# A new hand-written order for the same tasks on five queues, and an x tile that is given back by whichever reader is last

## The chip, the cores and the metric

The kernel runs on one core of one Trainium2 chip. The metric is device time in microseconds (us) of one execution; the kernel before the change has a median of 258.22 us over three executions (257.47 to 258.88). All inputs and the output lie in device memory as float32. The core has a matrix engine (PE, which also has a row of its own for loading weights, PEld), three engines for elementwise work (DVE, ACT, POOL), and SP, which here only issues transfers and a few register loads.

## The reference

```python
# q, k, v: (4, 8, 768, 64); sampled_blocks: (24, 3); x tokens: 3072 of width 512; d_ff = 2048
mask = |i_block - j_block| <= 1, or either block is the first or last of 24, or j_block is sampled for i_block
attn = softmax(where(mask, q @ k.T / 8, -1e9)) @ v            # (4, 8, 768, 64), blocks of 32 rows
x    = attn.transpose(0, 2, 1, 3).reshape(3072, 512)
out  = (relu(x @ w_in) ** 2) @ w_out                          # w_in 512 x 2048, w_out 2048 x 512
```

## The kernel before, in words

**Tasks and the order.** The body first makes 1224 tasks (class Task). Each holds a function that emits a few instructions, the tasks that must stand before it, the buffers it takes (get) and the buffers it gives back (put). Then `run_program` (line 92) walks through a hand-written list, PROGRAM: a word such as `A246`, `V25` or `P231/2` names an engine (P = PE, V = DVE, A = ACT, G = POOL, S = SP's transfer queue), a task number and, for a task that writes PSUM, one of four PSUM banks X. The order of words is the order of instructions on each queue. Buffers other than the banks are dealt round robin: pT (8, the exponentials), r (3, relu results), g (12, squares), xT (4, transposed x), VG (3), KG (2), ys (2, output rows) and others. `run_program` asserts that a buffer is free, in program order, when the next task takes it. What has to wait in time is left to semaphores between the engines.

**Attention, batches 0 and 1** (units 0 to 7, each two heads). For each unit, 256 queries and two key chunks of 128, `scores` makes a 128x1024 bank of scores on PE (through `pair`, line 203: two matmuls of 64 rows), `exps` (L360, ACT) turns it into a pT tile, `masks` (L367, DVE) multiplies by a 0/1 mask tile (queries 0 to 255 have the mask added on PE instead), `values` or `values_full` (L203, L398) multiplies by V, `normalize` (L410 reciprocal, L413 multiply, both DVE) divides by the sums. The mask tiles come from PE through `mask_evac`, on ACT (L277) or on DVE (L279). In batch 0 the result is transposed on PE (L427) and copied to xT; in batch 1 it goes to the tile XS and is transposed by a DMA (L440).

**Attention, batches 2 and 3** (units 8 to 15) reads only the sampled key blocks, two block pairs per visit: `v_gather` (an indirect DMA on POOL, L579, or plain DMAs on SP, L582, whose addresses come from registers), `k_gather` (L593 to L599, copies on DVE or POOL whose addresses come from registers), `s_scores`, `s_exps` (L623, ACT), `s_masks` (L630, DVE), `s_values` (L653, PE), `s_normalize` (L659, L662, DVE), `s_transp` (L666, DMA). The sampled numbers pass once through a small table: `table_masks` writes the mask MKS (casts, L123, DVE), and `table_rows` computes row numbers (L524) and then loads the block numbers into registers on POOL, DVE and SP (L561, a TENSOR_LOAD).

**The feed-forward part** works in twelve tiles of 256 tokens. A tile has four groups of `hidden` (f = 0, 4, 8, 12; four parts of 8 matmuls each) that read its xT tile and w_in, then `relu` (L707 ACT or L709 DVE), `square` (L718 ACT or L720 POOL; two halves in the first tile and the last two), `output` (eight parts; matmuls with w_out), `out_copy` (L121, L123) and `store` (L771 to L781). The last tile's output is cut in four: 128 tokens whole, then 128 tokens by 256, 128 and 128 columns, 256, 128, 64 and 64 KB; the third of the four (i == 2) is issued on ACT's queue, all other stores on SP's.

**Casts and loads.** float32 inputs are cast to bf16 by `cast_qk` and `cast_v` on DVE, POOL or ACT (all through `copy`, L121 and L123). The weights are loaded in eight pieces by POOL's queue, and two small transfers on SP (S82, S83) wait for two of them before the later loads.

Of the kernel before, what the change touches and what calls it, by code (L numbers as in the profile page):

```python
# [25 lines left out]
def kernel(  # L26
# [22 lines left out]
    NF = d_ff // P  # L49
# [741 lines left out]
    ev, cv, cq, sc_of, va_of, mu, mk, wl, gate, xb = {}, {}, {}, {}, {}, {}, {}, {}, {}, {}  # L791
# [152 lines left out]
    for us in [range(b * HP, (b + 1) * HP) for b in range(B)]:  # L944
# [11 lines left out]
        if us[0] >= SB * HP:  # L956
            b = us[0] // HP
# [8 lines left out]
    for T in TILES:  # L966
        b, c0, tw = T
        n_u = per_unit(T)
        need = [mu[b * HP + a, c0] for a in range(HP)] if b < SB else [mu['s', b, c0 // P + i] for i in range(2)]
        for f in range(0, NF, n_u):  # L970
# [17 lines left out]
        for i, y in enumerate(ys):  # L988
# [3 lines left out]
            for part in range(NY):  # L992
# [4 lines left out]
                           put=[gbuf[T, f] for f in fs if (T, f) in gbuf] if i == len(ys) - 1 and part >= NY // 2 else [])  # L997
# [4 lines left out]
        A29 G35 P4/3 V32 P30/0 P12/2 P14/3 P9/1 P5/1 V31 P33/1 V111 P36/3 P0/2 A37 V1 V34 P102/2 V209 V46 P47/0 P106/1 A103 V48 P104/3  # L1002
        V43 A107 P44/0 G57 P7/2 V45 A105 P58/1 V54 P113/0 V59 P55/2 A114 P117/3 G41 V56 P2/1 V67 A118 P115/2 V3 P108/0 A116 V64 P127/1
        V109 P10/3 P65/3 A128 P123/2 V66 A124 P68/1 P125/3 G75 V69 V63 P92/1 P110 A126 P133/2 G76 V112 A134 P137/3 G52 S28 S42 S18 S19
        V93 S20 P88/0 A138 G38 V155 V89 P84/1 P119/2 G74 V85 A60 P86/0 P39/3 P135/1 V120 G73 A87 V40 A136 P121 P61/0 G49 P129/3 V122
        V62 G77 V70 P176/2 P170/0 P139/1 A177 G81 V130 G80 A171 V140 P146/2 P131 V132 A147 P149/3 V172 P71/0 P141 V142 A150 V72 P50/2
        P173/1 V148 P781/0 A174 P782 V178 P189/3 P783 V51 A190 V175 P90/1 P15/2 P96/2 P784 V91 A97 P183/3 V151 A785 P94/2 P179/1 V95
        A184 G787 P143/0 P774/2 V180 P775 A144 V191 G78 P186/3 P181 P776 V182 A187 P777 V145 P157/0 V778 A786 P152/3 A158 P160/1 V188
        P788/2 A161 V153 P163/0 P789 V185 A164 P790 V162 P154 P217/1 P791 A156 V159 A218 P192/0 V165 P795/3 A792 V193 S82 P166/1 S83
        V296 V219 S53 S254 A779 G794 S253 P194 P100/2 A780 P796 V195 V167 A101 P214/0 P797 G793 A215 P168 P798 V169 P211/2 V799 P824/1  # L1010
        G79 A212 P825 P196/0 G256 V216 P826 A197 P199/3 P818/2 G801 S257 P827 A200 P819 V828 P202/0 A800 S261 P228/3 P820 G22 A203
        S262 P821 V213 P812/1 S269 A229 V822 P813 G258 P220/0 A829 P814 V201 P245/2 S259 P221 A246 V198 P815 P802/3 V222 A816 P231/2
        V266 P223 P803 A232 V204 S267 P239/1 V230 P804 A224 A240 V264 S270 P242/0 P205/2 V233 S265 A243 P225/1 P206 P805 V207 A226
        S277 V274 P288/0 S436 S255 P208 P806 V227 A289 S275 V247 P11/1 P291/1 A823 P234/0 V241 P807 A292 V210 V244 P98/2 P235 V272
        P808 A99 V236 A817 S273 P298/2 V290 P248/1 P237 A299 P809 V238 S278 V293 P285/0 S279 V300 P249 A810 P830/2 V250 P831 A286 V282
        P304/3 P251 P832 V260 A305 P301/0 V252 P833 S263 V287 P852/1 A302 S334 S283 V834 P853 P846/3 G280 P313/0 V303 P854 A314 P316/2
        S281 P855 P847 A317 V856 G284 P294/0 P848 A835 S271 P295 V306 P310/1 S21 P849 G268 V297 A311 P864/2 V318 P865 S440 A850 P307/0
        V315 P866 S438 A857 P308 G851 S446 P355/3 P867 V309 A356 P322/1 V868 P858/0 P859 A323 P349/3 V357 P325/2 P860 A350 V312 P861
        P836/1 V276 A326 V351 S456 P319/3 A862 P328/2 V327 S439 P320 S447 A329 V321 P352/0 P837 S811 V324 A353 S454 P339/2 V330 P838
        A340 V354 P331/3 P342/0 A869 S385 V341 P332 P358/2 V333 P839 A343 V23 S335 G441 P359 A863 P336/3 P361/0 G443 P840 A337 P841  # L1020
        G451 A362 S622 P364/3 G449 P842 A365 P373/0 G445 S450 P843 A374 G461 P870/3 A844 S444 P367/0 V338 P871 A368 V344 S463 P872
        V347 V360 S455 V366 S442 P376/0 P345/1 A377 V363 P379/2 P346 P873 S452 V348 A380 V369 P403/0 P874 A404 V375 S464 P370/2 V378
        P400/1 P393/0 V381 P371 A401 P875 V372 S471 S448 A394 V402 P382/1 P390/2 V405 P383 A391 P387/0 P876 V384 A388 V395 S386 P406/1
        P886/2 V392 A407 P887 V457 P427/0 P877 A428 V465 P24/1 P888 S497 S462 A878 G453 P889 V408 S458 P880/0 A890 P881 P430/3 S466
        P882 V27 G891 A431 P883 P409/2 A884 P926/3 V26 P927 A885 P410 G469 P415/0 V398 V25 P928 V411 G467 A416 P892/1 S608 V389 P424/2
        S879 P893 A425 P929 S468 V432 P894 A930 P895 V426 P396/0 S470 A896 P16/2 V429 P898/3 S845 P397 S616 A931 P418/2 P433/1 V399
        P899 V459 A419 P932/0 P933 V474 S460 P412/2 P900 A413 P901 V417 P934 A902 S473 P434 V420 P935 V435 P482/3 G903 P904/2 A483
        V936 A897 P492/1 P905 V414 A493 P914/3 G503 P915 P480/0 S499 S623 P421/1 A481 P916 S542 P422 P906 G472 V423 V484 P907 S437
        G937 P917 P487/1 P908 V918 A488 P477/1 P490/0 P909 G501 A478 V504 A491 P485/1 P920/3 A919 G543 V494 P921 V479 V621 P475/0 P910
        A486 G500 V489 V625 A476 P911 V613 P495/1 A912 G546 S632 S913 V547 P511/2 S607 P505/0 V496 P922 A512 S520 S502 P923 A506  # L1030
        P954/1 V924 G627 P955 P514/2 P508/0 P956 A515 V507 G524 P557/3 S545 P957 V513 A509 P948/2 A925 P949 S614 P938/0 G544 A558 S498
        P939 V516 A958 V525 P551/3 S523 P950 A552 P940 V510 P554/3 P951 A555 P548/1 P941 G589 S628 A549 P517/3 A952 P966/1 G959 V518
        A953 P967 P535/2 P942 V550 S519 A536 P529/3 P943 G521 S626 V559 P526/2 P944 V590 G522 A527 P945 V537 P968 V609 A946 P960/2
        P961 V556 A530 P969 V528 P532/0 P962 A970 S540 S615 V553 P963 S585 G586 S624 P988/3 A971 V964 P989 P560/1 A533 V531 P990 A965
        V534 P594/2 P994/0 V561 A595 P995 P991 G567 S562 P996 A992 P538/1 V619 V568 S631 A993 P597/3 P972/2 S606 V539 A598 P997 V596
        S541 P600/1 P973 A601 G587 P1000/3 A998 V617 S620 P974 G999 P975 S610 P572/1 P1001 A573 S630 P982/0 G637 P1002 S588 P1003
        P575/1 P983 V1004 A576 P976 V611 P984 P578/1 P569/3 P985 V629 S612 A570 P977 V599 A986 V633 P978 S563 G565 S618 A579 V602
# [51 lines left out]
```

## Time and profile before

One execution was profiled: it took 258.88 us as timed, and its span in the trace is 257.1 us, so 1.78 us lie outside the trace. The granted clock was 1.000.

| engine | busy, us | share of span | instructions |
|---|---|---|---|
| PE | 243.1 | 95% | 5265 |
| PEld | 182.1 | 71% | 5265 |
| ACT | 183.6 | 71% | 217 |
| DVE | 171.3 | 67% | 408 |
| POOL | 98.8 | 38% | 178 |

A row of the trace names a line, an engine, an operation and its tiles (out<-in) and how many instructions it stands for. "busy" counts a moment once even if several instructions overlap. Matmuls are pipelined: one lasts 269 ns for 256 columns, yet 14 of them in a row take 0.93 us from the first's start to the last's end. The share of busy time is a mean over stages whose limits differ, so a stage has to be read by itself. SPq, DVEq and ACTq are the engines' own queues, which issue transfers and register loads and are not counted as busy.

### The profile page before, as it was taken

The numbers are of one execution on the slowest core, as the hardware profiler recorded it, in microseconds if no ns is written. First come the engines' busy times: TensorE is split into PE (matmuls) and PEld (weight loads), VectorE is DVE, ScalarE is ACT, GpSimd is POOL, SyncE is SP. The second block draws the span as 40 slices with busy tenths as digits, with TensorE's granted clock in tenths as the row PEclk, the third lists the DMA queues.
The fourth block names the chain that finished last, engine by engine and source line by source line (L and its number), as shares of the span: only waits on it lengthen the run. The fifth ranks groups of instructions, "written<-read, shape, count | busy, mean of one in ns | idle before, by whom it ended". The sixth has DMA issues, their size and how long they took to land.

```text
span 257.1 us, 12061 instructions
## 1 busy us (share of the span) xinstructions
PE 243.1 (95%) x5265; PEld 182.1 (71%) x5265; DVE 171.3 (67%) x408; ACT 183.6 (71%) x217; POOL 98.8 (38%) x178
## 2 busy tenths in 40 slices
PE   7888999999999997998998999999999999999993
PEld 4667879678874677975864867866875677767683
DVE  7778988899889995969916756657536725730301
ACT  3899999998999797846783975675965286623640
POOL 3183247003316026198556314264357620412100
PEclk9999999999999999999999999999999999999999
DMA  6999989999999996999699779998474923044022
GB/s 200 374 250 207 206 205 155 270 202 252 250 281 179 197 202 153 340 229 154 188 243 202 194 174 167 251 214 199 129 206 95 189 40 60 5 121 148 23 86 83
DMA packets 64692, 47.08 MB, mean 183 GB/s; under 512 B 31567, under 2 KB 60624, under 8 KB 64640
## 3 DMA queue, kind: packets, MB, share of 16 engines
q1 hardware_dynamic: 58512, 37.82, 64.7%
q0 software_dynamic: 5440, 8.05, 16.8%
q8 instruction: 41, 0.67, 1.1%
q10 hardware_dynamic: 688, 0.46, 0.6%
q14 instruction: 11, 0.09, 0.1%
HBM read 35.51 MB, written 7.91 MB: 169 GB/s over the span
## 4 chain that ended last, share of the span: by engine, by line
PE 53%; DVE 5%; DVEq 1%; issue 1%; ACT 1%; ACTq 0%
PE X L203 49%; PE X L653 4%; DVE VB L123 1%; ACT pT L623 1%; DVEq L561 1%; DVE MKS L123 1%; DVE pT L630 1%; DVE r L709 0%; DVE KG L599 0%; DVE qc L123 0%; DVE XS L413 0%; DVE KG L593 0%; DVE XS L662 0%; DVEq L599 0%; DVE rs L410 0%
## 5 line engine op out<-in xcount | busy, mean ns | idle before, releaser
L203 PE MATMUL X<-xT,w_in_sb 64*128 64x256 bf16 x1536 | 100.8, 269 | 2.8 <-issue 1.5
L203 PE MATMUL X<-w_out_sb,g 64*128 64x512 bf16 (+3 forms) x960 | 95.2, 334 | 0.1
L203 PEld LDWEIGHTS <-w_in_sb 64*128 64x128 bf16 x1536 | 74.6, 94 | 16.0 <-issue 5.4
L360 ACT ACTIVATE pT<-X 128x1024 bf16<-128x1024 f32 x72 | 70.6, 1030 | 7.6 <-PE X L203 6.8
L623 ACT ACTIVATE pT<-X 128x768 bf16<-128x768 f32 (+1 forms) x56 | 41.6, 766 | 26.5 <-PE X L203 23.9
L203 PEld LDWEIGHTS <-g 64*128 64x128 bf16 x960 | 40.3, 94 | 26.3 <-PE X L203 0.4
L720 POOL TENSOR_TENSOR g<-r 128x1024 bf16<-128x1024 f32 (+1 forms) x20 | 31.6, 1587 | 64.4 <-ACT r L707 47.2
L707 ACT ACTIVATE r<-X 128x1024 f32<-128x1024 f32 x28 | 29.8, 1068 | 20.6 <-PE X L203 20.5
L709 DVE TENSOR_SCALAR r<-X 128x1024 f32<-128x1024 f32 x20 | 24.5, 1224 | 26.7 <-PE X L203 13.7
L367 DVE TENSOR_TENSOR pT<-pT,VG 128x1024 bf16<-128x1024 bf16 x60 | 40.9, 715 | 0.2
L718 ACT ACTIVATE g<-r 128x1024 bf16<-128x1024 f32 (+1 forms) x40 | 35.2, 899 | 2.7 <-DVE r L709 2.5
L203 PE MATMUL X<-QKT 64*128 64x256 bf16 (+1 forms) x384 | 31.6, 250 | 3.3 <-DVE XS L413 1.3
L630 DVE TENSOR_TENSOR pT<-pT,MKS 128x768 bf16<-128x768 bf16 (+1 forms) x48 | 27.6, 607 | 10.7 <-ACT pT L623 10.5
L203 PEld LDWEIGHTS <-QKT 64*128 64x128 bf16 x384 | 16.7, 95 | 9.5 <-issue 4.1
L579 POOL DMA_INDIRECT VG<-rows,idx x19 | 20.2, 1061 | 4.4 <-issue 2.6
L203 PEld LDWEIGHTS <-pT 64*128 64x128 bf16 x768 | 16.0, 94 | 1.9
L203 PE MATMUL X<-VB,pT 64*128 64x65 bf16 x768 | 17.1, 190 | 0.0
L203 PEld LDWEIGHTS <-KG 64*128 64x128 bf16 x528 | 13.8, 95 | 4.5 <-issue 0.2
L659 DVE RECIPROCAL ss<-X 128x8 f32<-128x8 f32 x12 | 2.5, 206 | 19.5 <-PE X L653 17.3
L653 PEld LDWEIGHTS <-pT 128*64 128x64 bf16 x624 | 11.9, 111 | 4.9 <-issue 3.7
L203 PE MATMUL X<-QKT,KG 64*128 64x64 bf16 x528 | 15.3, 190 | 0.1
L123 POOL CAST VB<-vs 128x768 bf16<-128x768 f32 x9 | 7.8, 869 | 16.5 <-DMA vs<-in_v_dram 16.4
(107 smaller groups left out, 210.3 us busy)
## 6 DMA issues: line engine op xcount, KB each, us to landing
vs<-in_v_dram SPq DMA_DIRECT2D x14, 384.0 KB
ks<-in_k_dram SPq DMA_DIRECT2D x13, 384.0 KB
qs<-in_q_dram SPq DMA_DIRECT2D x12, 384.0 KB
out_dram<-ys SPq DMA_DIRECT2D x9, 512.0 KB
VG<-rows SPq DMA_DIRECT2D x20, 132.0 KB
w_in_sb<-in_moe_w_in_dram POOLq DMA_DIRECT2D x4, 512.0 KB, 8.6
w_out_sb<-in_moe_w_out_dram POOLq DMA_DIRECT2D x4, 512.0 KB, 9.9
rows<-VB SPq DMA_DIRECT2D x2, 792.0 KB
```

The lines of the kernel that those rows point to most:

```text
L123: (V if e == "DVE" else G).tensor_copy(out=out, in_=in_)
L203: last = nc.tensor.matmul(out(r ^ crossed), lhsT(r ^ crossed, rows), rhs(r ^ crossed, rows), skip_group_check=True, **kw)
L360: A.activation(out=pT[:, :, 0:n], in_=stile.pop(a)[:, :, 0:n], func=AF.Exp, scale=scale)
L367: V.tensor_tensor(out=pT, in0=pT, in1=m[:, None].broadcast_to([P, 2, len(cs), w]), op=AOP.mult)
L579: G.indirect_dma_start(out=to[0:RS * HB], out_offset=None, in_=pairs, in_offset=bass.IndirectOffsetOnAxis(ap=idx[0:RS * HB, g - 1:g], axis=0))
L623: A.activation(out=pT[:, :, 0:n], in_=stile.pop((u, v, gs))[:, :, 0:n], func=AF.Exp, scale=scale)
L630: V.tensor_tensor(out=pT, in0=pT, in1=m[:, None].broadcast_to([P, 2, n]), op=AOP.mult)
L653: nc.tensor.matmul(po[i * D:(i + 1) * D, h, a * VW:(a + 1) * VW], pts[g][:, h, c * D:(c + 1) * D], val, start=a == 0 and c == 0, stop=c == ...
L707: A.activation(out=to, in_=src, func=AF.Relu)
L709: V.tensor_scalar(out=to, in0=src, scalar1=0.0, scalar2=None, op0=AOP.max)
L718: A.activation(out=g, in_=r, func=AF.Square)
L720: (G if e == "POOL" else V).tensor_mul(out=g, in0=r, in1=r)
```

## The change

The change has two parts. The first is a condition in the code that makes the hidden tasks: the xT tile is now given back by the last part of each of the four groups, not only by that of the group f = 12, so it is free when all four have gone. Nothing on the chip depends on this by itself; it lets the four groups stand in any order in PROGRAM. The second is a new PROGRAM: the same 1224 tasks in another order, some on another engine or in another bank. The diff, with the first and last lines of PROGRAM:

```diff
-                             put=[xb[b, c0]] if f + n_u == NF and end else []))
+                             put=[xb[b, c0]] if end else []))
...
     PROGRAM = """
-        A29 G35 P4/3 V32 P30/0 P12/2 P14/3 P9/1 P5/1 V31 P33/1 V111 P36/3 P0/2 A37 V1 V34 P102/2 V209 V46 P47/0 P106/1 A103 V48 P104/3
...
-        P1221 P1211 A1222 S1223 V1212 S1213
+        P4/0 G35 G46 V28 G52 G80 A111 A29 G73 G75 G22 G77 G74 G63 A209 P2/1 P0/2 G81 G76 P14/3 V42 V3 V1 S82 P36/0 A37 P18 G155 P30/3
...
+        P1201 P1219 P1220 P1221 A1222 P16/0 V1202 P8/2 S1223 S1213 P13/0 S1203 P15/2 P10/0 S1155 S1193
```

PE does the same matmuls. Tasks that change engine: four relus go from DVE to ACT (28 to 32 on ACT, 20 to 16 on DVE); five half squares go from POOL to ACT (15 to 20 on ACT, 9 to 4 on POOL); two mask evacuations go from ACT to DVE (4 to 2), and two copies to xT from DVE to ACT; one cast of 128x512 leaves ACT. About sixteen casts of inputs go from DVE to POOL (for instance V tiles 5 to 3 on DVE and 9 to 11 on POOL). Four of the V gathers go from POOL (19 to 15) to SP (3 to 7), which makes 42 plain DMAs on SP's queue in place of 18, and six register loads on SP in place of three.

**Around exponential A246, on PE and ACT.** A246 is the exponential of unit 3, queries 512 to 767, keys 512 to 767. In both programs the scores P231 of unit 2 take the bank that A246 frees. Before, A246 is the 46th task of ACT that computes, and 838 matmuls stand ahead of P231 on PE; among their tasks are 28 parts of hidden (8 matmuls each), 1 part of output (8), 32 scores, 8 x transposes (4 each) and 8 of warming (2 each). In the changed program A246 is the 47th, and 788 matmuls stand ahead of P231: 22 parts of hidden, none of output, 33 scores, 9 x transposes and 7 of warming, the rest as before. That is 48 hidden, 8 output and 2 warming matmuls fewer, and 4 score matmuls and 4 transposes more. ACT's list up to A246 was, before, 32 exponentials (A246 among them), 2 casts, 3 mask evacuations, 2 relus, 4 half squares and a whole one, 1 evacuation of keys and 1 copy to xT; it is now 33 exponentials, 1 cast, 2 mask evacuations, 2 relus, 6 half squares, 1 evacuation of keys and 2 copies to xT.

The start of ACT's list, before (qc is a cast input, QKT the transposed keys and queries, X a PSUM bank, pT an exponential):

```order
L169 DMA ks_77<-in_k_dram 128x2x192 x2
L179 ACT_TABLE_LOAD
L121 CAST qc_106<-ks_77 128x384
L121 COPY QKT<-X_149 128x2x2x64
L360 ACTIVATE pT_86<-X_148 128x1024
L360 ACTIVATE pT_87<-X_147 128x1024
L360 ACTIVATE pT_88<-X_149 128x1024
```

and in the changed program (VG here holds a mask tile):

```order
L169 DMA ks_77<-in_k_dram 128x2x192 x2
L179 ACT_TABLE_LOAD
L121 CAST qc_108<-ks_77 128x384
L121 COPY QKT<-X_146 128x2x2x64
L277 ACTIVATE VG_208<-X_149 128x512
L277 ACTIVATE VG_207<-X_148 128x512
L360 ACTIVATE pT_86<-X_149 128x1024
L360 ACTIVATE pT_87<-X_147 128x1024
```

Two mask evacuations now stand ahead of the first exponential on ACT; the first of them needs a cast of 512 columns on DVE and a mask matmul on PE.

**Where the register loads stand, on DVE.** Before, after the last of batch 1's first casts (MKS is the mask of the sampled batches, tab the table of block numbers):

```order
L367 TENSOR_TENSOR pT_87<-pT_87,VG_208 128x1024
L123 CAST MKS<-X_147 128x5x64 x3
L123 CAST MKS<-X_147 128x6x64 x3
L524 TENSOR_SCALAR idx<-X_147,lane 128x11
L561 TENSOR_LOAD tab x6
L410 RECIPROCAL rs<-X_148 128x4
L413 TENSOR_TENSOR XS<-X_148,rs 128x2x2x64
```

and in the changed program:

```order
L367 TENSOR_TENSOR pT_86<-pT_86,VG_208 128x1024
L524 TENSOR_SCALAR idx<-X_149,lane 128x11
L561 TENSOR_LOAD tab x6
L367 TENSOR_TENSOR pT_88<-pT_88,VG_208 128x1024
L367 TENSOR_TENSOR pT_87<-pT_87,VG_208 128x1024
L593 COPY KG_118<-QKT 128x4x64
```

The register loads now stand ahead of two mask multiplications and the first K gather, and the MKS casts behind that gather. On PE, the feed-forward parts P898 to P892 of the first batch (output and hidden, some 40 matmuls) now stand between `table_spread`, which fills the bank that these loads read, and the scores P424, which take the bank that the following normalization (V411) frees; before, two parts (P928, P892) stood there.

**The end of SP's list.** Before:

```order
L666 DMA_TRANSPOSE xT_116<-XS 128x4x128 x2
L776 DMA out_dram<-ys_85 128x2x512
L776 DMA out_dram<-ys_84 128x2x512
L779 DMA out_dram<-ys_85 32x512 x2
L779 DMA out_dram<-ys_85 64x512
L781 DMA out_dram<-ys_85 128x512
L776 DMA out_dram<-ys_84 128x2x512
L776 DMA out_dram<-ys_85 128x512
L776 DMA out_dram<-qs_74 128x256
L776 DMA out_dram<-qs_76 128x128
```

and in the changed program:

```order
L666 DMA_TRANSPOSE xT_117<-XS 128x4x128 x2
L779 DMA out_dram<-ys_85 32x512 x2
L779 DMA out_dram<-ys_85 64x512
L781 DMA out_dram<-ys_85 128x512
L776 DMA out_dram<-ys_84 128x2x512
L776 DMA out_dram<-qs_76 128x128
L776 DMA out_dram<-qs_74 128x256
L776 DMA out_dram<-ys_84 128x2x512
L776 DMA out_dram<-ys_85 128x512
```

The row qs_76 128x128 is the store S1223 of the last piece of the last tile (64 KB), which waits for the last output copy, A1222. Before, it closes the list; now the stores of 128 KB, 512 KB (the eleventh tile) and 256 KB stand behind it.

More of the change, by code (lines that the diff above doesn't have):

```diff
@@ L1006 @@
[L1006 to L1017, printed above, removed]
@@ L1054 @@
[L1054 to L1056 removed]
+        P4/0 G35 G46 V28 G52 G80 A111 A29 G73 G75 G22 G77 G74 G63 A209 P2/1 P0/2 G81 G76 P14/3 V42 V3 V1 S82 P36/0 A37 P18 G155 P30/3
+        V19 P17/1 V31 P86/1 V32 S53 P47/2 P92/3 V87 P33/0 P84/1 V48 V34 A93 P88/2 A89 P11/3 P106/3 V43 A107 P44/0 V85 P9/2 V45 V54
```

92 lines of the change are left out of this document (51 added, 41 removed).

## The prediction, made before the result was known

> **What bounds the kernel now.** I read the engine totals first, then the busy time by stretches, then the waits of ACT and PE, then the chain of waits. The page's first part and the stretches:
>
> ```profile
> PE 243.1 (95%) x5265; PEld 182.1 (71%) x5265; DVE 171.3 (67%) x408; ACT 183.6 (71%) x217; POOL 98.8 (38%) x178
> ...
> 7.00:46.00 39.00, 36.07 (x771) 29.54 (x769) 32.85 (x68) 37.73 (x45) 18.09 (x30) 1.00 1.08 234
> ...
> 61.00:97.00 36.00, 35.39 (x809) 26.02 (x803) 33.49 (x80) 33.62 (x36) 11.43 (x16) 1.00 1.11 218
> 97.00:125.00 28.00, 25.55 (x614) 20.78 (x614) 22.07 (x57) 18.69 (x23) 17.00 (x30) 1.00 0.91 204
> 125.00:150.00 25.00, 23.27 (x538) 17.51 (x539) 15.21 (x45) 17.84 (x22) 12.41 (x27) 1.00 0.95 211
> 150.00:253.30 103.30, 102.94 (x2152) 73.37 (x2148) 48.89 (x114) 59.50 (x76) 37.36 (x63) 1.00 0.58 133
> 253.30:257.10 3.80, 0.00 (x0) 0.00 (x0) 0.29 (x1) 0.18 (x1) 0.00 (x0) 1.00 0.13 37
> ```
>
> The columns after the stretch are its length and the busy time of PE, PEld, DVE, ACT, POOL. Over the whole span PE is the bound: the same matmuls have to run after the change. What can change is PE's time without work, 257.1 − 243.1 = 14.0 us: 2.93 from 7 to 46 us, 0.61 from 61 to 97, 2.45 to 125, 1.73 to 150, 0.36 to 253.3, the 3.8 us tail, and 2.1 in the stretches left out (the start and 46 to 61). But PE's share hides a second bound: from 7 to 46 us ACT has 37.73 of 39.00 us busy, more than PE, and ACT waited for PE only 2.0 us up to 61 us:
>
> ```profile
> ACT pT L360 <- PE X L203: 2.0, 4, 0.9
> ...
> 6.93 2.85 ACT L360 ACTIVATE pT<-X 128x1024 bf16<-128x1024 f32 x3 [0.88 <-PE X L203]
> ...
> 44.66 1.02 ACT L360 ACTIVATE pT<-X 128x1024 bf16<-128x1024 f32 x1
> ...
> 46.05 0.40 PE L203 MATMUL X<-QKT 64*128 64x256 bf16 x4
> ```
>
> The first row is the wait; the next two are from ACT's timeline, the last from PE's. The row at 44.66 is A246, which frees the bank for the four score matmuls at 46.05 (P231). So, up to there, the front runs at ACT's pace, and how much PE gets done meanwhile depends on what stands in PE's list ahead of the scores that ACT feeds.
>
> After 61 us PE is short of work only in a few places:
>
> ```profile
> PE X L203 <- issue: 1.5, 4, 0.4
> PE X L203 <- DVE XS L413: 1.3, 2, 1.0
> PE X L653 <- issue: 0.6, 2, 0.4
> PE X L203 <- ACT pT L623: 0.5, 1, 0.5
> PE X L203 <- DMA xT<-XS: 0.4, 1, 0.4
> PE X L653 <- ACT pT L623: 0.3, 1, 0.3
> PE X L203 <- DVE XS L662: 0.2, 1, 0.2
> ```
>
> Six waits for another engine make 2.7 us; six gaps with no visible wait ("issue") make 2.1.
>
> **Term 1, the front: +4.0 us.** The marker is A246 and P231 behind it. PE's work ahead of P231 falls by 48 hidden, 8 output and 2 warming matmuls and rises by 4 score matmuls and 4 transposes. Their costs, from PE's groups up to 46 us (count | busy, mean ns of one), and a row of PE's timeline where hidden runs undisturbed:
>
> ```profile
> L203 PE MATMUL X<-xT,w_in_sb 64*128 64x256 bf16 x224 | 15.4, 269 | 0.1
> L203 PE MATMUL X<-w_out_sb,g 64*128 64x512 bf16 x8 | 1.0, 376 | 0.0
> ...
> 241.80 0.93 PE L203 MATMUL X<-xT,w_in_sb 64*128 64x256 bf16 x14
> ```
>
> By the first row a hidden matmul takes 15.4/224 = 69 ns of PE's time. With the warming matmuls, scores and transposes at the same price, 48 + 2 − 4 − 4 = 42 of them make 2.9 us, and the output part 1.0: 3.9. But groups overlap one another, so this is the upper bound. By the third row 14 matmuls take 0.93 us of which the last lasts 0.269, so they follow one another every (0.93 − 0.269)/13 = 51 ns: 42 make 2.1, and the output part scaled likewise 0.7: 2.9, the lower bound (it neglects what a switch between forms costs). I take 3.3, a little nearer the lower, since the front switches forms often but overlaps them too. That much PE work moves behind a point that ACT sets; it isn't lost itself, but PE's idle time ahead of the point grows by it.
>
> Does ACT reach A246 sooner? ACT's groups up to 46 us:
>
> ```profile
> L718 ACT ACTIVATE g<-r 128x512 bf16<-128x512 f32 x4 | 2.4, 633 | 0.0
> L277 ACT ACTIVATE VG<-X 128x512 bf16<-128x512 f32 x3 | 1.8, 610 | 0.0
> L718 ACT ACTIVATE g<-r 128x1024 bf16<-128x1024 f32 x1 | 1.1, 1075 | 0.0
> L121 ACT CAST qc<-qs 128x512 bf16<-128x512 f32 x1 | 0.7, 650 | 0.0
> L121 ACT COPY xT<-X 128x256 bf16<-128x256 bf16 x1 | 0.4, 372 | 0.0
> ```
>
> It gains an exponential (+1.02, the row above), two half squares (+1.27) and an xT copy (+0.37), and loses a whole square (−1.08), a cast (−0.65) and a mask evacuation (−0.61): +0.3 us. Two mask evacuations now stand ahead of its first exponential. They are work moved forward, but they wait for a cast of 512 columns and a mask matmul, while before ACT began at 6.93 us, as soon as its first scores were there. Below, the start is not later at all (0); above, two evacuations pass in series without cover, 2 × 0.61 = 1.2. I take +0.4, nearer the lower end because ACT waited 0.88 us there already. Sum 3.3 + 0.3 + 0.4 = +4.0, with bounds 3.2 (2.9 + 0.3) and 5.4.
>
> **Term 2, the tail: +2.1 us.** A row of SP's queue, and two stretches (DMA GB/s last):
>
> ```profile
> 228.90 1.08 SPq L776 DMA_DIRECT2D out_dram<-ys  x2
> ...
> 230.00:231.00 1.00, 1.00 (x14) 0.45 (x10) 1.00 (x1) 0.97 (x2) 0.00 (x0) 1.00 1.03 362
> 231.00:232.00 1.00, 1.00 (x12) 0.42 (x10) 0.14 (x1) 0.75 (x2) 0.78 (x1) 1.00 1.00 375
> ```
>
> Before, the only transfers issued after the last output copy are 64 KB on SP and 64 KB on ACT's queue, and the tail is 3.8 us. In the new list S1223, which waits for that copy, stands ahead of 128, 512 and 256 KB: 1024 KB leave after the end of PE's work in place of 128. Two stores of 512 KB, issued at 228.90, moved at 362 and 375 GB/s two us later. The extra 896 KB (0.918 MB) at 0.37 MB/us take 2.5 us. Some of it fills time in which the small stores' issue and landing left the queues idle: I take 2.1. Bounds: 1.5 (1 us is covered) and 3.0 (nothing is covered, and one issue of 1.08/2 = 0.54 us stands in series). Nothing hides it, as no work comes after.
>
> **Term 3, the middle gives back: −3.9 us.** PE now comes to the work that it did at 61 us some 4 us later, while the work of DVE and POOL ahead of it is not later. The costliest of the six waits sit at the end of this chain:
>
> ```profile
> 95.23 0.40 DVEq L561
> ...
> 96.49 0.46 DVEq L561
> ...
> 98.18 0.94 DVEq L561
> ...
> 99.20 0.86 DVEq L561
> ...
> 100.21 0.19 DVE rs L410
> 100.43 0.43 DVE XS L413
> 100.91 12.49 PE X L203 x318
> ```
>
> Register loads of 0.4 to 0.94 us stand on DVE ahead of the normalization that frees PE's bank. In the new order they stand ahead of two masks and a gather, and PE has some 40 feed-forward matmuls (some 4 us at 0.07 to 0.13 each, as above) between the table and the scores that need that bank, where it had 16: cover. The new stall could be the normalization behind the MKS casts, which follow a K gather; the same 4 us cover it. Each such wait also drains PE's pipeline: a matmul lasts 269 ns where they follow each other every 51 to 69, so the true price of a wait is about 0.2 us above the row. If all six go: 2.7 + 6 × 0.2 = 3.9. The six "issue" gaps I leave in place: nothing in the order of matmuls removes them. Bounds: 0 (other waits come in their place) and 2.7 + 2.1 + 12 × 0.2 = 7.2 (the gaps go too).
>
> **Other edits, at 0.** Moved casts lie on POOL, which is busy 11.43 of 36 us and 17.00 of 28; the cover is that DVE's own queue, 33.49 of 36 us busy, gets shorter: each cast that leaves it takes 0.55 us with it. The price if the cover fails is rival D. SP's V gathers: 24 more plain DMAs and three more register loads on a queue that otherwise only issues; at 1.08/2 = 0.54 us for an issue (the row of term 2) they take some 15 us of SP over the sampled visits, spread over 100 us; if one came late it would show as a wait of L653 for a DMA, and no such wait is among those above. The four relus and five half squares on ACT after 61 us: ACT has 59.50 of 103.30 us busy there. The condition on the x tile issues nothing.
>
> **Sum.** 4.0 + 2.1 − 3.9 = +2.2. On the profiled execution's 258.88 (span 257.1 and 1.78 outside) that is 261.1; on the median, 258.22, it is **260.4 us**.
>
> **The rivals.**
>
> *B, the middle gives nothing back*: for the six old waits, others come in DVE's or SP's new order. For it: DVE still has 33.49 of 36 us busy from 61 to 97. Against: PE comes 4 us later, more than any single wait (1.0). 258.2 + 4.0 + 2.1 = 264.3.
>
> *C, the other side*: late DVE is behind all of PE's idle time after 61 us, the issue gaps too, and the lighter DVE (sixteen casts of 0.55 make 8.8 us, four relus go as well, two evacuations come) takes all of it away. Place: PE from 61 to 150 us; price −7.2. With the low ends of front and tail (3.2, 1.5) it makes 258.2 + 4.7 − 7.2 = 255.7, with their middles 257.1. It decides from the point where more than 4.7 + 1.3 = 6.0 of the 7.2 us go. For it: from 150 us on, where DVE is busy for only 48.89 of 103.30 us, PE stands idle for 0.36. Against: from 61 to 97 us DVE is fullest and PE idle for only 0.61; and the profile names no releaser for them.
>
> *D, POOL holds DVE.* With POOL idle a mask takes less than beside POOL's casts (groups from 46 to 60 and from 60 to 66 us), and one cast beside a K gather took 2.62 us where its like took 0.55:
>
> ```profile
> L367 DVE TENSOR_TENSOR pT<-pT,VG 128x1024 bf16<-128x1024 bf16 x11 | 7.2, 684 | 0.0
> L367 DVE TENSOR_TENSOR pT<-pT,VG 128x1024 bf16<-128x1024 bf16 x4 | 3.4, 864 | 0.0
> 118.63 0.55 DVE L123 CAST VB<-vs 128x768 bf16<-128x768 f32 x1
> 120.29 2.62 DVE L123 CAST VB<-vs 128x768 bf16<-128x768 f32 x1
> ```
>
> Sixteen casts more on POOL would cost DVE from 16 × 0.18 = 2.9 us, if each meets one mask, upward. Spread over a stage that DVE nearly bounds, that takes back most of term 3: 260.4 + 2.9 = 263.3. Against: the DVE work that leaves, 8.8 us, is three times as much. The Trainium skill, SBUF — State Buffer, "Who interferes with whom", states a rule that speaks against this change: the port pair that DVE and GpSimd share is taken as an exclusive lock, so the loser waits out the whole instruction, and a tensor_tensor with both inputs in SBUF contends with a GpSimd instruction that reads SBUF. The trace agrees in kind (864 against 684 ns), not in a full block each time.
>
> **How the numbers follow.** A measurement of this kernel can tell about 0.5%, 1.3 us, from no change: faster is below 256.9, slower above 259.5. Chances: the forecast 0.50 (its own range 258 to 262.5), B 0.13, C 0.27, D 0.10. Of C, 0.20 falls below 256.9 and 0.07 within; of the forecast, 0.04 below, 0.17 within and 0.29 above; B and D are above. So faster 0.24, same 0.24, slower 0.52. The range reaches from C's low end, 255.5, to B's, 264.5.
>
> **What would show it.** Term 1: the four score matmuls behind A246 start near 46.5 us (0.3 + 0.4 later) with some 50 matmuls fewer ahead of them, and PE's idle time from 7 to 46 us is near 6.5 us (2.93 + 3.3 + 0.3), not 2.93. If ACT instead has gaps there, the bound is another. Term 2: more than 5 us between PE's last matmul and the span's end, with over 300 GB/s in two of them. Term 3: the waits for XS L413 gone or under 0.5 us, PE's idle time from 61 to 150 us near 2 us in place of 4.8; with B, new waits of over 2 us there; with D, masks (L367, L630) with a longer mean than before. I would be wrong outright if PE stood no more idle before 46 us than it did.

## The result and the profile after

The changed kernel is slower by 5.3%: a median of 272.74 us against 258.55 us for the kernel before beside it, a ratio of 1.053 (95% interval 1.044 to 1.062). Measured once more, beside the experiments, it was 1.047 (1.038 to 1.057). Ratios leave out executions that took over 1.5% longer than the fastest of the same kernel. The forecast was 260.4 us, in a range from 255.5 to 264.5.

The span of the profiled execution grew from 257.1 to 270.8 us, by 13.7. The first part of the page and the busy time by stretches of the changed kernel (length, then PE, PEld, DVE, ACT, POOL, granted clock, DMA share, GB/s):

```profile
PE 245.6 (91%) x5265; PEld 185.6 (69%) x5265; DVE 163.1 (60%) x389; ACT 188.8 (70%) x225; POOL 104.3 (39%) x185
...
7.00:46.00 39.00, 35.25 (x750) 28.29 (x752) 32.97 (x73) 38.18 (x47) 13.63 (x25) 1.00 1.16 255
...
61.00:97.00 36.00, 30.30 (x625) 22.46 (x623) 23.78 (x61) 27.48 (x31) 14.25 (x20) 0.95 1.12 234
97.00:125.00 28.00, 23.53 (x553) 20.46 (x546) 17.43 (x44) 19.96 (x21) 6.55 (x14) 0.94 0.58 152
125.00:150.00 25.00, 23.93 (x571) 17.16 (x565) 15.13 (x46) 17.66 (x25) 12.01 (x29) 1.00 0.92 173
```

PE's time without work grew from 14.0 to 270.8 − 245.6 = 25.2 us, by 11.2; the other 2.5 us are PE itself, which was busy for 245.6 in place of 243.1 us with the same matmuls. The largest part of the growth lies between 61 and 125 us: 5.70 + 4.47 = 10.2 us without work where it was 3.1, so 7.1 more. The end of the span adds 2.0, the stretches up to 61 us 1.2, and those from 125 us to the last output 0.8. The front, where the prediction put its largest cost, shows only 3.75 us from 7 to 46, against 2.93 before and 6.5 forecast.

The waits of PE name three places:

```profile
PE X L203 <- DVE XS L413: 5.7, 1, 5.7
PE X L203 <- DVE MKS L123: 2.3, 1, 2.3
PE X L203 <- DVE pT L367: 2.0, 1, 2.0
```

These are 10.0 us in three stalls. The first, in the timelines of PE, DVE, POOL and SP's queue:

```profile
88.34 0.84 PE L203 MATMUL X<-VB,pT 64*128 64x65 bf16 x24 [5.71 <-DVE XS L413]
...
75.67 0.42 DVE L413 TENSOR_TENSOR XS<-X,rs 128x256 bf16<-128x256 f32 x1
...
78.99 0.17 DVE L410 RECIPROCAL rs<-X 128x4 f32<-128x4 f32 x1
87.86 0.42 DVE L413 TENSOR_TENSOR XS<-X,rs 128x256 bf16<-128x256 f32 x1 [8.71 <-DMA xT<-XS]
...
76.14 1.22 SPq L312 DMA_TRANSPOSE QKT<-qc  x1
77.48 0.94 SPq L149 DMA_DIRECT2D vs<-in_v_dram  x1
78.53 0.56 SPq L771 DMA_DIRECT2D out_dram<-ys  x1
79.64 1.52 SPq L312 DMA_TRANSPOSE QKT<-qc  x1
81.28 0.52 SPq L149 DMA_DIRECT2D vs<-in_v_dram  x1
81.89 2.65 SPq L440 DMA_TRANSPOSE xT<-XS  x2
...
80.19 0.83 POOL L123 CAST VB<-vs 128x768 bf16<-128x768 f32 x1 [0.31 <-DMA vs<-in_v_dram]
```

At 76.1 us the fourth normalization of batch 1's first 256 tokens is done, and the transposing transfer of its x tile (S335, L440) could go. On SP's queue two transposes, two loads and a store stand ahead of it, and the last of these issues at 81.28, 0.3 us after a cast on POOL (the last row) has ended; the chain of waits runs through that cast and the load that it waited for. The transfer goes at 81.89 and lands before 87.9. Until then DVE can't write the next normalization to the tile XS, so it stands still for 8.7 us, the bank that this normalization frees stays taken, and PE waits 5.7 us for the bank. Before the change the same transfer was issued at 75.86, at once, and DVE asked for XS only at 84.22:

```profile
75.86 2.52 SPq L440 DMA_TRANSPOSE xT<-XS  x2
...
84.22 0.42 DVE L413 TENSOR_TENSOR XS<-X,rs 128x256 bf16<-128x256 f32 x1
```

The second and third stall, on DVE and on PE's side of it:

```profile
103.90 0.22 DVE L524 TENSOR_SCALAR idx<-X,lane 128x11 int32<-128x11 f32 x1
108.66 1.29 DVE L367 TENSOR_TENSOR pT<-pT,VG 128x1024 bf16<-128x1024 bf16 x2 [4.54 <-ACT r L707]
...
110.89 2.67 DVE L123 CAST MKS<-X 128x384 bf16<-128x384 f32 x6
...
109.41 0.29 PE L203 MATMUL X<-VB,pT 64*128 64x65 bf16 x8 [2.02 <-DVE pT L367]
113.61 0.39 PE L203 MATMUL X<-QKT 64*128 64x256 bf16 x4 [2.31 <-DVE MKS L123]
```

DVE stands idle for 4.54 us. The releaser that the trace names, a relu on ACT, is not what this mask reads; but the six register loads stand between these rows, and by the view of that line they take

```profile
L561 DVEq TENSOR_LOAD <-tab x6: 801/819/1071, 102.8 to 107.8; - x6
```

(shortest, median and longest in ns, first and last start): the last starts at 107.8 and ends when DVE goes on. They now have only short work queued on DVE ahead of them. PE runs out at 107.4, because its values need a mask that stands behind the loads. It runs out again at 111.3 for the scores P427, which take the bank that the table of the sampled numbers fills and the six casts of MKS empty. PE goes on at 113.61, as soon as the casts end at 113.56; the normalization behind them multiplies only at 113.68.

The 2.5 us of longer busy time follow the stalls. Stretches of 1 us, with the granted clock after the busy times, and two rows of PE:

```profile
87.00:88.00 1.00, 0.00 (x0) 0.00 (x0) 0.14 (x1) 0.00 (x0) 0.00 (x0) 0.82 1.28 285
88.00:89.00 1.00, 0.66 (x25) 0.65 (x26) 0.95 (x5) 0.00 (x0) 0.00 (x0) 0.50 0.68 132
...
90.00:91.00 1.00, 1.00 (x8) 0.35 (x4) 0.86 (x6) 0.00 (x0) 0.00 (x0) 0.50 1.27 326
91.00:92.00 1.00, 1.00 (x16) 0.61 (x14) 0.96 (x9) 0.00 (x0) 0.00 (x0) 0.98 2.13 149
...
115.00:116.00 1.00, 1.00 (x14) 0.92 (x10) 0.96 (x3) 0.98 (x2) 0.70 (x1) 0.50 0.86 180
...
118.00:119.00 1.00, 1.00 (x14) 0.77 (x12) 0.30 (x1) 1.00 (x2) 1.00 (x6) 0.82 1.18 438
...
88.97 2.93 PE L203 MATMUL X<-w_out_sb,g 64*128 64x512 bf16 x16
...
98.04 1.90 PE L203 MATMUL X<-w_out_sb,g 64*128 64x512 bf16 x16
```

The granted clock falls to 0.50 at about 87.6 us (0.82 is the mean of its stretch), 5.0 us after PE's last matmul (82.6), and stays there for 3.4 us, to about 91.0, while PE has resumed at 88.3. It does the same after the two shorter stalls, from 115.0 to 118.4 us. 16 output matmuls took 2.93 us, mostly at the low clock, and 1.90 us ten us later. Before the change no stretch was below 1.00. The Trainium skill, TensorE: Matmul & The Clock Gate, "Part 1: The HAM clock gate (the "warmup" mystery)", states that the clock has two levels, half and full, set by PE's activity in windows of about 3.4 us, and shows a case where it fell 5.2 us after the last matmul. The trace agrees: 0.50 and 1.00, low times of 3.4 us, and 5.0 us from 82.6 to 87.6.

These sizes vary between executions. In the second trace of the changed kernel the first wait is 6.5 us and the clock is at 0.50 for 6.8 us behind it, but it stays at 1.00 after the shorter waits of 2.0 and 2.3 us; PE's busy time is 244.8 us there, 1.7 more than before the change.

The end went as forecast. SP's queue of the changed kernel:

```profile
265.05 0.83 SPq L776 DMA_DIRECT2D out_dram<-qs  x2
265.93 0.98 SPq L776 DMA_DIRECT2D out_dram<-ys  x2
```

PE's last output matmul ends at 264.7, the span at 270.8: 6.1 us, where it was 3.8.

### The profile page after: what moved, and what is told of

Its sections match the earlier page's. It is cut to its first block, busy times and chain, and to the rows that moved or that the text cites. A ratio compares the mean times of both kernels' runs of the same rounds, so it can differ in the third digit from the quotient of the medians.

```text
span 270.8 us, 12145 instructions
## 1 busy us (share of the span) xinstructions
PE 245.6 (91%) x5265; PEld 185.6 (69%) x5265; DVE 163.1 (60%) x389; ACT 188.8 (70%) x225; POOL 104.3 (39%) x185
## 4 chain that ended last, share of the span: by engine, by line
PE 65%; DMA 11%; DVE 7%; ACT 4%; SPq 4%; POOL 3%; issue 3%; DVEq 2%; POOLq 0%; ACTq 0%
PE X L203 57%; DMA ks<-in_k_dram 5%; PE X L653 5%; ACT pT L360 3%; DMA QKT<-qc 2%; PE X L398 2%; SPq L312 2%; POOL qc L123 2%; DMA vs<-in_v_dram 2%; DVEq L561 2%; DMA xT<-XS 2%; DVE pT L367 1%; POOL VB L123 1%; DVE MKS L123 1%; SPq L149 1%
## 5 line engine op out<-in xcount | busy, mean ns | idle before, releaser
L623 ACT ACTIVATE pT<-X 128x768 bf16<-128x768 f32 (+1 forms) x56 | 41.1, 764 | 28.5 <-PE X L203 27.4
L367 DVE TENSOR_TENSOR pT<-pT,VG 128x1024 bf16<-128x1024 bf16 x60 | 43.3, 752 | 7.4 <-ACT r L707 4.5
L718 ACT ACTIVATE g<-r 128x1024 bf16<-128x1024 f32 (+1 forms) x45 | 38.2, 872 | 6.9 <-DVE r L709 6.6
L720 POOL TENSOR_TENSOR g<-r 128x1024 bf16<-128x1024 f32 (+1 forms) x15 | 25.3, 1689 | 44.9 <-DVE r L709 31.9
L707 ACT ACTIVATE r<-X 128x1024 f32<-128x1024 f32 x32 | 34.2, 1076 | 10.8 <-PE X L203 10.7
L630 DVE TENSOR_TENSOR pT<-pT,MKS 128x768 bf16<-128x768 bf16 (+1 forms) x48 | 30.0, 658 | 18.9 <-ACT pT L623 17.7
L709 DVE TENSOR_SCALAR r<-X 128x1024 f32<-128x1024 f32 x16 | 19.6, 1222 | 25.1 <-PE X L203 23.0
L123 POOL CAST VB<-vs 128x768 bf16<-128x768 f32 x11 | 10.2, 932 | 42.3 <-DMA vs<-in_v_dram 17.0
L123 POOL CAST qc<-qs 128x384 bf16<-128x384 f32 (+2 forms) x18 | 13.3, 757 | 18.2 <-DMA qs<-in_q_dram 17.0
L579 POOL DMA_INDIRECT VG<-rows,idx x15 | 14.6, 971 | 8.5 <-PE X L653 6.2
L123 POOL CAST qc<-ks 128x384 bf16<-128x384 f32 (+1 forms) x16 | 10.6, 680 | 18.3 <-PE X L203 14.4
```

Source lines behind the costliest of these rows:

```text
L123: (V if e == "DVE" else G).tensor_copy(out=out, in_=in_)
L367: V.tensor_tensor(out=pT, in0=pT, in1=m[:, None].broadcast_to([P, 2, len(cs), w]), op=AOP.mult)
L579: G.indirect_dma_start(out=to[0:RS * HB], out_offset=None, in_=pairs, in_offset=bass.IndirectOffsetOnAxis(ap=idx[0:RS * HB, g - 1:g], axis=0))
L623: A.activation(out=pT[:, :, 0:n], in_=stile.pop((u, v, gs))[:, :, 0:n], func=AF.Exp, scale=scale)
L630: V.tensor_tensor(out=pT, in0=pT, in1=m[:, None].broadcast_to([P, 2, n]), op=AOP.mult)
L707: A.activation(out=to, in_=src, func=AF.Relu)
```

## The experiments

The kernels ran in four sets on three chips (the first and the last set on the same one), and the kernel before had medians of 257.1 to 261.8 us on them; so ratios to the kernel before beside each are compared, and 1% between sets is not much more than the intervals. The sets were: experiments 1 to 4; 5 (first), 6, 7 and the changed kernel once more; 9 and 5 (second); 8 and 10. In the diffs each line is a place in PROGRAM.

**1. The x tile's transfer first on SP's queue.**

```diff
 # order of SP's words around S335
-  S456 ... S811 ... S458 ... S464 ... V321 P359 P859 V341 S335
+  V321 S335 S456 S811 S458 S464 G461 P359 P859 V341
```

> The changed kernel, with the transposing transfer of batch 1's first x tile (S335) moved on SP's queue from behind two loads, a store and a transpose (S456, S811, S458, S464) to right behind the normalization that it needs; one cast of V (G461) moves behind them. Theory 1 (a queue that runs in order): S335 was issued at 81.9 us although its last input was there at 76.1, because those four stood ahead; DVE then waited 8.7 us for the tile XS and PE 5.7 us. It should now be issued near 77.5: 4.4 us earlier, the wait of PE at XS L413 falls from 5.7 to about 1.3 us, the clock that was 0.62 from 88 to 92 us stays near 1.00 (1.3 us more). Median near 267 us, 5.5 less than the changed kernel. Rival (the DMA engines are full there, so xT lands at the same time whatever stands first): the wait stays above 4 us, median above 271.

Measured: ratio 1.027 (1.019 to 1.035), against 1.053 and 1.047 for the changed kernel: 2 to 2.6% less, 5 to 7 us. In its trace the transfer leaves 3.2 us earlier and PE's wait is 0.8 us at this place:

```profile
77.35 1.21 SPq L312 DMA_TRANSPOSE QKT<-qc  x1
78.68 3.85 SPq L440 DMA_TRANSPOSE xT<-XS  x2
...
84.81 0.54 PE L203 MATMUL X<-VB,pT 64*128 64x65 bf16 x24 [0.82 <-DVE XS L413]
...
88.00:92.00 4.00, 3.57 (x43) 2.19 (x41) 3.86 (x20) 3.50 (x5) 0.00 (x0) 1.00 1.07 160
```

The transfers are the same ones and the DMA engines as full (a share of 1.21 from 74 to 88 us in both traces), so it is what stands ahead on the queue and not the load on the engines. The edit passes the other transfers and the wait for POOL's cast together, and no run separates the two. The clock stays at 1.00 from 88 to 92 us where it was 0.62. This is the largest single cause.

**2. The register loads behind the casts.**

```diff
 # order of DVE's words
-  V25 V408 ... V420 V474 ... V26 ... V27 V411
+  V408 ... V420 V26 V27 V25 ... V411 V474
```

> The changed kernel, with the register loads of the table (V25) moved on DVE behind two masks and the six casts of MKS (V26, V27), as before the change, and the first K gather (V474) behind the normalization V411. Theory 2: the six register loads of 0.8 us each run ahead of the elementwise work only if such work is queued in front of them; with 4 us of it in front, DVE's idle time of 4.5 us at 104 to 109 us falls to about 1.5, PE's waits of 2.0 and 2.3 us there fall below 1 us together, and the clock of 0.71 to 0.87 between 112 and 120 us goes back to 1.00. Median near 268 us, 4 to 5 less than the changed kernel. Rival (the loads cost the same in either place, the wait only moves to the normalization or the gather): less than 1.5 us gained, median above 271.

Measured: ratio 1.044 (1.036 to 1.052), 0.3 to 0.9% less than the changed kernel, about 1 to 2 us where 4 to 5 were expected. The waits did what the theory says. The two of 2.0 and 2.3 us are gone, and DVE's idle time there is now PE's doing:

```profile
DVE rs L410 <- PE X L203: 3.8, 3, 1.6
```

But PE got other gaps in place of them, at points that wait for nothing the profile shows:

```profile
127.70 1.04 PE L203 MATMUL X<-w_out_sb,g 64*128 64x512 bf16 x8 [1.72 <-issue]
134.64 0.22 PE L653 MATMUL X<-VB,pT 128*64 128x65 bf16 x1 [1.05 <-issue]
152.56 0.23 PE L203 MATMUL X<-QKT,KG 64*128 64x64 bf16 x4 [1.50 <-issue]
```

In the second trace of the changed kernel PE's waits from 40 to 254 us sum to 14.4 us, 4.8 of them for these masks and casts; here they sum to 14.1, with 0.3 for masks, but 4.5 in place of 0.8 at "issue" and 7.5 in place of 6.5 for XS L413. So the wait was located rightly, and its removal paid for less than half. Experiment 8 below tells what it is worth beside the other two edits.

**3. The stores in the old order, at the end.**

```diff
-  S1223 S1213 ... S1203 ... S1155 S1193
+  S1155 S1193 S1203 S1223 S1213
```

> The changed kernel, with the stores of 512, 256 and 128 KB (S1155, S1193, S1203) put ahead of the last 64 KB store (S1223) on SP's queue, which is all that changes. Term 2 of the prediction: 2.1 us less, median 270.6, and the time from PE's last matmul to the end of the span falls from 6.1 to about 4 us. Rival (the end is set by the fixed time of the last store, and the big ones go beside it): less than 0.7 us.

Measured: ratio 1.038 (1.029 to 1.047), 0.9 to 1.6% less. In its trace PE's last output matmul ends at 266.2 and the span at 270.3: 4.1 us, 2.0 less than the 6.1 of the changed kernel. Term 2 is confirmed in size by the trace. The rest of the difference in the ratios may lie between the sets; no run shows it.

**4. The casts back on DVE.**

```diff
-  G260 G264 G266 G272 G274 G276 G282 G457 G459 G465
+  V260 V264 V266 V272 V274 V276 V282 V457 V459 V465
```

> The changed kernel, with ten casts of units 4 to 7, 10 and 11 put back from POOL to DVE (V260, V264, V266, V272, V274, V276, V282, V457, V459, V465), at the same places in the list. Rival D and the theory that slow casts on POOL (0.83 to 1.3 us against 0.55) hold up SP's transposes (SP waited 13.7 us for POOL's casts between 30 and 110 us): SP comes to S335 earlier, the wait of PE at XS L413 falls by 3 us or more, median 267 to 269. Theory 1 (the order of SP's queue alone): the wait stays above 4 us, and DVE is longer by 10 casts of 0.55; median 272 to 275.

Measured: ratio 1.134 (1.126 to 1.142), far slower, which neither theory had expected. One row of DVE says why:

```profile
45.34 0.56 DVE L123 CAST qc<-qs 128x768 bf16<-128x768 f32 x1 [20.27 <-DMA qs<-in_q_dram]
```

In the new order these casts stand early in the list, ahead of what their loads allow. On POOL, with little else to do, such a cast waits for its load without holding up a mask or a normalization. On DVE it stops the normalizations and masks behind it for 20 us. So the kernel does not test rival D, but it shows that the move to POOL and the early place in the list belong together.

**5. All three edits.**

```diff
 # the edits of 1, 2 and 3 together
```

> The changed kernel with all three edits: the x tile's transfer ahead of the four others on SP, the register loads behind the MKS casts, the big last stores ahead of the last small one. If the three are separate causes and add up, 1.053 falls by the 2.65% of the first, about 0.9% of the second and 0.8% of the third to about 1.01 (262 us). What is left over the kernel before is then the front (term 1, predicted 4.0 us, seen as 0.8 us of PE's idle time so far) and gaps in the middle. Rival (the wait of one edit hides that of another, so that they do not add): above 1.025.

Measured: 1.008 (0.999 to 1.017), and in another set 1.019 (1.013 to 1.025). The first ratio rests on three executions of ten, the second on six of six. The three edits together take away 3 to 4 of the 5 per cent; one by one they took 2 to 2.6, 0.3 to 0.9 and 0.9 to 1.6, so within these margins they add up. What is left is 2 to 5 us. The second measurement had this expectation:

> The changed kernel with the three edits and its own front, once more beside the kernel with the old front, on one chip: a ratio to the kernel before of 1.005 to 1.02, as measured.

Part of what is left is in the front. PE's groups of matmuls up to 61 us that differ in count, of the kernel before:

```profile
L203 PE MATMUL X<-xT,w_in_sb 64*128 64x256 bf16 x285 | 19.4, 269 | 0.1
L203 PE MATMUL X<-QKT 64*128 64x256 bf16 x172 | 17.9, 270 | 2.0 <-DVE R L123 0.5 <-DVE xT L123 0.4 <-DVE QKT L123 0.3
L203 PE MATMUL X<-w_out_sb,g 64*128 64x512 bf16 x64 | 8.4, 376 | 0.0
```

and of the kernel with the three edits (second measurement; the changed kernel itself has 264, 168 and 54):

```profile
L203 PE MATMUL X<-QKT 64*128 64x256 bf16 x168 | 18.0, 277 | 0.5 <-DVE xT L123 0.2 <-ACT pT L360 0.2
L203 PE MATMUL X<-xT,w_in_sb 64*128 64x256 bf16 x264 | 17.7, 269 | 0.4 <-ACT pT L360 0.4
L203 PE MATMUL X<-w_out_sb,g 64*128 64x512 bf16 x50 | 6.4, 376 | 0.0
```

At 61 us PE has done 21 hidden, 4 score and 14 output matmuls fewer. At the prediction's two prices for hidden and scores (69 and 51 ns), and 8.4/64 = 131 ns for an output matmul or 97 ns in the same proportion, that is 2.6 to 3.6 us; for the changed kernel, with 10 output matmuls fewer, 2.2 to 3.0. But from 61 to 150 us PE is still idle for 6.5 us (second measurement) where it was 4.8 before the change, 1.9 of it in one gap marked "issue".

**The changed kernel once more**, in the same set as the first measurement of experiment 5:

> The changed kernel itself, unchanged, beside the three others of this set, so that they are compared on one chip. About 5% above the kernel before: the first measurement gave a ratio of 1.053.

Measured: the 1.047 given above.

**6. The wait put into the kernel before.**

```diff
 # PROGRAM of the kernel before
-  S335 ... S622 ... S450 ... S444
+  S622 ... S450 ... S444 S335
```

> The kernel before, with one word moved: batch 1's first x transfer (S335) stands on SP's queue behind a load and two transposes of batch 2 (S622, S450, S444) instead of ahead of them, as such transposes stand ahead of it in the changed kernel. Theory 1: it is issued near 81 us in place of 75.9 and lands near 86, while DVE wants the tile XS at 84.2; the wait appears at XS L413, 2 us or more, part of it on PE, and with the later tasks behind it the kernel is 1 to 4 us slower (ratio 1.005 to 1.015). Rival (only the changed kernel's DVE order makes the wait, which asks for XS at 79.2 us already): no difference that can be measured.

Only one run can be compared: 262.5 us beside a median of 260.5 for the kernel before. That leans to the theory and proves nothing about the time. The trace is of an execution of 268.3 us, too long to be compared, but it shows the wait that the edit was to make:

```profile
85.68 2.76 SPq L440 DMA_TRANSPOSE xT<-XS  x2
...
90.27 0.61 PE L203 MATMUL X<-QKT 64*128 64x256 bf16 x4 [3.06 <-DVE XS L413]
```

DVE waits 2.8 us for the transfer, which it did not wait for at all in the kernel before.

**7. The new tail in the kernel before.**

```diff
 # PROGRAM of the kernel before, end
-  S1155 ... S1193 ... S1203 ... S1223 ... S1213
+  S1223 S1213 S1203 S1155 S1193
```

> The kernel before with the last five stores in the changed kernel's order (64 KB first, then 128, 512 and 256 KB behind it on SP). Term 2 alone: 2.1 us more (ratio 1.008), nearly all between PE's last matmul and the end of the span: from 3.8 to about 5.9 us. Rival (they drain side by side): under 0.7 us.

Measured: ratio 1.011 (1.001 to 1.020), 0.3 to 5 us: slower, in keeping with 2.1 us, which alone would be 1.008. In its trace the last output matmul ends 6.0 us before the span does, where it was 3.8.

**8. Two edits, without that of the register loads.**

```diff
 # the edits of 1 and 3 together
```

> The changed kernel with the x tile first and the tail as before, without the edit of the register loads: what that edit is worth when the other stalls are gone. Theory 2 (the loads without cover cost 4 us): 4 us above the kernel with all three edits, ratio 1.025 to 1.035. Rival (most of that wait only moves to later gaps): 0.5 to 2 us above it, ratio 1.015 to 1.022.

Measured: 1.032 (1.025 to 1.039), against 1.008 and 1.019 with all three: the edit of the register loads is worth 1.3 to 2.4% here, 3 to 6 us, as theory 2 has it. But experiment 1, which also lacks it and has the slow tail on top, gave 1.027, so the value is uncertain by about a per cent; alone it was worth 1 to 2 us. Nor is the first stall always gone: the execution that was profiled here, the longest of the six (269.3 us), still has a wait of 3.6 us for XS L413. That the edit counts for more when the first stall is gone is likely, but not shown.

**9. The old front ahead of the new rest.**

```diff
 # first 270 words from the kernel before, the rest from experiment 5
-  P4/0 G35 G46 V28 ... S455 P242/2
+  A29 G35 P4/3 V32 ... V204 S267 P239/1
```

> The front by itself: the first 270 words of PROGRAM (up to about 46 us, past exponential A246 and scores P231) are those of the kernel before, in its order and on its engines; all later words are those of the changed kernel with the three edits (x tile first on SP, register loads behind the casts, tail as before). Compared with the same kernel with the new front, in this set. By the sum of PE's matmuls done at 61 us (by count of each form and the spacing of the undisturbed rows) the new front is behind by 2.6 us, against 4.0 in the prediction: this kernel should be 2 to 3 us faster than the one with the new front (about 258 to 260 where that one takes 261 to 262). If it is 4 us faster, term 1 was right in size; if under 1 us, the front costs nothing that isn't made up later. What still separates it from the kernel before is then the middle: faster than before if the new middle gives time back once its stalls are gone.

Measured: 1.027 (1.022 to 1.033), slower than the kernel with the new front (1.019), where 2 to 3 us faster was expected. The graft has a stall of its own, right behind the cut:

```profile
46.00:61.00 15.00, 11.50 (x274) 8.64 (x272) 9.19 (x19) 11.12 (x14) 6.33 (x7) 1.00 1.10 239
...
49.98 1.14 PE L203 MATMUL X<-VB,pT 64*128 64x65 bf16 x48 [1.81 <-ACT xT L121]
```

PE stands idle for 3.5 of these 15 us. A likely reason, not tried apart, is that the new rest follows loads and casts that the new front had issued sooner and the old front had not. So this does not measure the front alone; the new front and the new rest belong together.

**10. The filler taken from the front of the kernel before.**

```diff
 # PROGRAM of the kernel before
-  P820 ... P821 P812/1 ... V822 P813 ... P814 ... P245/2 ... P815 P802/3 ... A816 P231/2
+  P245/1 ... P231/1 P820 P821 V822 P812/2 P813 P814 P815 P802/3 A816
```

> The kernel before, with six parts of hidden and the one of output (P820, P821, P812 to P815, P802: 56 matmuls) moved on PE from ahead of scores P231 to right behind it, with the two relus that follow them; ACT's list up to exponential A246 stays as it was. This is term 1's removal of filler and nothing else of the new front. Term 1: A246 comes when it came (45.7 us at most 0.5 earlier), and the 2.9 to 4 us of PE work behind it are late: 2 to 3 us slower (ratio 1.008 to 1.012). Rival (PE makes them up in slack that its busy time hides): within 1 us, ratio under 1.004.

Measured: 1.027 (1.017 to 1.037), 4.4 to 9.5 us slower, more than expected. In its trace:

```profile
7.00:46.00 39.00, 33.26 (x719) 26.64 (x720) 32.64 (x68) 37.22 (x44) 18.10 (x30) 1.00 1.08 233
46.00:61.00 15.00, 13.01 (x198) 8.40 (x199) 6.94 (x13) 7.11 (x9) 0.00 (x0) 0.77 0.73 174
...
46.16 0.50 PE L203 MATMUL X<-QKT 64*128 64x256 bf16 x4 [1.64 <-ACT pT L360]
```

The scores P231 start at 46.16 us with 56 matmuls fewer ahead of them, and at 46.05 us with them: here ACT sets that point, as term 1 says. PE's idle time from 7 to 46 us is 5.74 in place of 2.93 us, 2.8 more. Behind the point the block of 56 matmuls keeps the next scores from ACT (busy for 7.11 of 15 us), and the clock falls to 0.77; the rest of the loss is put down to these two, which no run separates. That second part is of this experiment's making; the changed kernel spreads its matmuls.

## Why the prediction was wrong

The forecast was the right sign of a result that is six times as large. By its own steps:

- **Term 1, the front, +4.0: the mechanism right, the size too large.** Experiment 10 shows that ACT sets the start of P231 once filler is taken away ahead of it, and that this becomes idle time (2.8 us for 56 matmuls). With the filler in place the point was PE's by a little: A246 ended at 45.68, and PE's own list kept P231 until 46.05. At 61 us the changed kernel is behind by 2.2 to 3.0 us of matmuls. The part that was mis-sized is ACT's: the prediction added 0.3 us of work and 0.4 of a later start; the first exponential did start later (8.77 in place of 6.93 us), but ACT then ran almost without a gap, and P231 started at 45.19, 0.9 us earlier than before. With 3.3 for the moved matmuls that makes 2.4. The sign to look for was wrong too: PE's idle time from 7 to 46 us rose by 0.8 us, not 3.6. Part of the slack hides in the busy time of pipelined matmuls: up to 61 us the same 66 mask matmuls (X<-R,oh) and 96 transposes (L305) are busy for 8.3 and 4.2 us in place of 8.0 and 3.7. The count of matmuls shows what the idle time does not.
- **Term 2, the tail, +2.1: right.** 6.1 against 3.8 us by the trace, 2.0 back when the order is restored, and 2.2 more when the new order is put into the kernel before.
- **Term 3, the middle, −3.9: wrong in sign, and the step that failed.** Most of the old waits did go (those for ACT's L623 grew from 0.8 to 1.3 us, and the "issue" gaps fell from 2.1 to 1.0), but the sum supposed that none would come in their place. Three came, of 10.0 us, and PE's busy time grew by 2.5 us at the slower clock behind them.
- **"SP's V gathers ... at 0" and "the cover is that DVE's own queue gets shorter": the gap in the working.** These sentences priced SP's and POOL's added work by its length. What counted was what stands ahead of what on SP's in-order queue. The prediction followed SP's list at its end and at its gathers, not at the one transfer on which DVE's tile XS hangs. In the new order transposes, loads and a store stand ahead of it, and the last of them goes only after a cast on POOL. The order of SP's words and the old trace (S335 issued at 75.86, 0.06 us after its input) would have shown it.
- **The register loads: seen, but the cover was wrong.** The prediction set some 4 us of feed-forward matmuls against them. The loads cost 4.5 us of DVE's idle time where they had cost 2.7 (97.5 to 100.2 us), because before the change the casts of MKS stood ahead of them on DVE and about half of the loads ran under those casts. The casts moved behind the loads, so load and cast now add up. Nor was the wait behind the casts for the normalization, as the prediction had it, but for the bank that the casts themselves read. The loads, too, were read too short: 0.40 to 0.94 us are pieces of the chain of waits, and each whole load took 0.86 to 1.07 us in the kernel before.
- **The rivals.** B, that others come in place of the old waits, named what happened, at a chance of 0.13, but priced the new waits like the old ones, at 264.3 us. D's sign did appear: the mean of a mask rose from 715 to 752 ns (60 of L367) and from 613 to 698 ns (the 40 wide ones of L630), and fell from 577 to 461 ns for 8 narrow ones, some 4.7 us in sum, on an engine whose busy time fell by 8 us. But of PE's long waits only that of 2.0 us names a mask, and that mask stood behind the register loads; so the trace speaks against D as the cause, and no run tests it alone. C did not occur.

What stays open: the gaps marked "issue" that appear once the register loads are covered (1.0 to 1.7 us each in experiment 2); how the 2 to 5 us that experiment 5 leaves divide between the front and these gaps; and how much of the transfer's delay is the length of the queue and how much the cast on POOL.

## What to carry to other kernels

When an order is changed on several queues, follow for each queue that runs in order the transfers and tiles on which another engine waits, and list what now stands ahead of them; the sum of a queue's work says nothing of that. A wait that is hidden because of its place (register loads under casts, a cast that waits for its load on an idle engine) is lost when its neighbours move, even if neither changes. Price a stall of PE of some microseconds at more than its length: here PE's busy time grew by 2.5 us on 10.0 us of waits in one trace, and by 1.7 us in another.

## What the runs showed of the hardware

- After PE had stood still for 5.7 us, the granted clock was 0.50 for 3.4 us, and for as long again after two stalls of 2.0 and 2.3 us within some 6 us, there only from 1.4 us after PE had resumed. This is not the same each time: in the second trace of the changed kernel a wait of 6.5 us brought 6.8 us at 0.50 and the two shorter ones none, and in experiment 1, with the first wait cut to 0.8 us, the clock stayed at 1.00 there but was at 0.50 for 6.8 us after the two shorter ones (1.9 us each).
- Six register loads on DVE had medians of 0.8 to 1.0 us each wherever they stood, but cost DVE 4.5 us of idle time with next to nothing queued ahead and 2.7 us behind casts of 2.7 us; behind two masks and the same casts DVE waited for PE and not for them.
- A cast that waited for its load held DVE for 20.3 us, and the kernel lost about 8% by it and the nine others; on POOL, which had little else to do, the same casts held up no mask and no normalization.
